# Attention steps of a fused attention and mixture kernel: weighted sums and output transposes ahead of the query transposes, which get two PSUM banks of their own

## The chip, the core and the metric

The kernel runs on one core of one Trainium2 chip. The metric is device time in microseconds; three runs of the kernel before took 1943.64 to 1944.79 us, with a median of 1944.15 us. A profile records one further execution. Engines are called TensorE (PE in the rows; PEld are its weight loads), VectorE (DVE), ScalarE (ACT), GpSimd (POOL) and SyncE (SP, which here issues loads and stores).

## What is computed

Three layers follow each other: linear attention with an exponential feature map, then a mixture of experts with soft weights, then one in which each token goes to one expert. The change touches the first alone:

```python
def _attn_ref(q, k, v, w_phi):
    def phi(x):
        proj = np.einsum('bhsd,df->bhsf', x, w_phi)
        proj = proj - np.max(np.abs(proj), axis=-1, keepdims=True)
        return np.concatenate([np.exp(proj), np.exp(-proj)], axis=-1)
    q_p, k_p = (phi(q), phi(k))
    kv = np.einsum('bhsf,bhsd->bhfd', k_p, v)
    z = np.sum(k_p, axis=2)
    num = np.einsum('bhsf,bhfd->bhsd', q_p, kv)
    den = np.einsum('bhsf,bhf->bhs', q_p, z)[..., None] + 1e-06
    return num / den
```

with 4 batches, 8 heads, 576 positions, 64 values per head and 128 features, all in float32.

## The kernel before

Attention's work is cut into 8 units (two batches and two heads each) of 3 groups; a group is 3 chunks of 128 positions for both heads. The order is written out by hand: the loop from line 651 calls `step` once per group (step i takes group i as keys), and each engine executes its instructions in the order of these calls. Each group passes through a pipeline:

- `proj` (L138) multiplies a group of keys (step i) or queries (two steps later) by the feature matrix on TensorE (L144, row tiles of 64), and VectorE takes the largest magnitude (L149) and subtracts it (L150; `mk`, `prk` for keys, `mq`, `prq` for queries). For keys ScalarE takes both exponentials at once (`ek`, L154).
- `kvm` (L159), one step later, sums the products of key features and values in two banks, psC and psB (L170, column tiles of 64). It issues 24 matmuls, or 32 in the middle group of a unit, where a chunk spans two batches (steps 5, 8, 11, ..., 23). Each float32 matmul stands in the profile as two weight loads and two matmuls, except transposes: 48 or 64 records. After the last group of a unit `kvcopy` copies the sums out (ScalarE).
- `qtr` (L178), one step after a query's projection, transposes it (6 transposes, L184), and ScalarE takes the exponentials (`eq`, L187).
- `num` (L190), one step after that, makes the weighted sums and their denominators (L198, 48 records, column tiles of 64). VectorE divides: an addition, a reciprocal and a multiply (L201 to L203; the multiply writes `xn`). This document calls these three the division.
- `xtr` (L206), again one step later, transposes the quotient (3 transposes, L211), ScalarE copies it out (`xo`, L213) and SyncE stores it.

PSUM has 8 banks. Tiles psR (two banks each, two buffers) serve the key projection, the query projection and the query transposes in turn; psD (one bank, two buffers) serves weighted sums and output transposes; psC and psB hold the key-value sums. Steps from i = 25 on, the tail, run in a new pool, whose first tiles psC and psB lie on the old pool's first two banks and where each user has tiles of its own; there the first matmuls of the next layer (`more`) are put between the parts. Small VectorE work (`misc_comp`) is called ahead of steps 6 and later, four transposes of the expert embedding (`misc_trans`, L296) after step 11, and background work (`bg`: weight and input splits on ScalarE and GpSimd) after the steps from 12 on.

Of the kernel before, what the change touches and what calls it, by code (L numbers as in the profile page):

```python
# [11 lines left out]
F32 = mybir.dt.float32  # L12
# [9 lines left out]
B, H, S, D = 4, 8, 576, 64  # L22
NT = B * S
DM = H * D
E, FF = 8, 1024
P = 128
NTL = NT // P
KD = DM // P
# [16 lines left out]
def build(tc, a, out):  # L45
# [5 lines left out]
    live = {}  # L51
# [9 lines left out]

    n_ps = [0]

    def psum(tag, shape):
        n_ps[0] += 1
        bufs = {"A": 4, "B": 1, "C": 1, "D": 2}[tag]
        return live["pp"].tile(shape, F32, tag="ps" + tag, bufs=bufs, name=f"ps{tag}{n_ps[0]}")
# [31 lines left out]
    NG, NC = len(CH), len(CH[0])  # L99
    GW = NC * P  # L100
    S2 = 2 * S
    W = D + 1
# [13 lines left out]

    def heads2(tags):
        if not live.get("tail"):
            n_ps[0] += 1
            t = live["pp"].tile([P, 2, 512], F32, tag="psR", bufs=2, name=f"psR{n_ps[0]}")[:, :, 0:GW]  # L120
            return [t[:, 0], t[:, 1]], [(slice(0, 2), t)]
        ts = [psum(t_, [P, 1, GW]) for t_ in tags]
        return [t[:, 0] for t in ts], [(slice(h_, h_ + 1), t) for h_, t in enumerate(ts)]

    def warm(n):
        ps = psum("D", [P, P])
        for _ in range(n):
            T.matmul(ps, ident, ident, start=True, stop=True)

# [4 lines left out]
    load_in(0, "k", 1)  # L134
    load_v(0)
    warm(10)

    def proj(u, which, g):  # L138
        r = live.pop(("r" + which, u, g))
        hs, parts = heads2("CB")  # L140
        for c in range(NC):
            for h_ in range(2):
                rs = slice(h_ * D, h_ * D + D)
                T.matmul(hs[h_][:, c * P:(c + 1) * P], r[rs, c * P:(c + 1) * P], wphi[rs, :], start=True, stop=True)  # L144
        m = ap_.tile([P, 2, NC], F32, tag="m", bufs=4, name=f"m{which}{u}{g}")
        pr = ap_.tile([P, 2, NC, P], F32, tag="pr" + which, name=f"pr{which}{u}{g}")
        for h_, ps in parts:
            ps = ps.rearrange("p h (c f) -> p h c f", f=P)
            V.tensor_reduce(out=m[:, h_], in_=ps, axis=AX.X, op=ALU.max, apply_absolute_value=True)  # L149
            V.tensor_tensor(out=pr[:, h_], in0=ps, in1=m[:, h_].unsqueeze(3).to_broadcast([P, h_.stop - h_.start, NC, P]), op=ALU.subtract)  # L150
        if which == "k":
            ek = ap_.tile([P, 2, 2, NC, P], F32, tag="ek", name=f"ek{u}{g}")
            for sg in range(2):
                A.activation(out=ek[:, sg], in_=pr, func=AF.Exp, scale=1.0 - 2.0 * sg)  # L154
            live["ek", u, g] = ek
        else:
            live["pr", u, g] = pr

    def kvm(u, g):  # L159
        v, ek = live["v", u], live.pop(("ek", u, g))  # L160
        if g == 0:
            live["kv", u] = [psum(t, [P, 2, 2 * W]) for t in "CB"]
        for ci, c in enumerate(CH[g]):
            for sg in range(2):
                for h_ in range(2):
                    ps = live["kv", u][h_]
                    for s0 in (c,) if c < 4 else (4, 5) if c == 4 else (c + 1,):
                        o = W * (s0 > 4)
                        for cs in HALVES:
                            T.matmul(ps[cs, sg, o:o + W], ek[:, sg, h_, ci, cs], v[:, h_, s0 * W:s0 * W + W], start=(c == 0 and sg == 0), stop=(c == 8 and sg == 1))  # L170

    def kvcopy(u):
        kvz = ap_.tile([P, 2, 2, 2 * W], F32, tag="kvz", name=f"kvz{u}")
        for h_, ps in enumerate(live.pop(("kv", u))):
            A.copy(kvz[:, h_], ps)
        live["kvz", u] = kvz

    def qtr(u, g):  # L178
        pr = live.pop(("pr", u, g))
        eq = ap_.tile([P, 2, 2, GW], F32, tag="eq", name=f"eq{u}{g}")  # L180
        hs, parts = heads2("DD")
        for h_ in range(2):
            for c in range(NC):
                T.transpose(hs[h_][:, c * P:(c + 1) * P], pr[:, h_, c, :], ident)  # L184
        for sg in range(2):
            for h_, ps in parts:
                A.activation(out=eq[:, sg, h_], in_=ps, func=AF.Exp, scale=1.0 - 2.0 * sg)  # L187
        live["eq", u, g] = eq

    def num(u, g):  # L190
        eq, kvz = live.pop(("eq", u, g)), live["kvz", u]
        ps = psum("C" if live.get("tail") else "D", [P, 2 * NC, W])
        for ci, c in enumerate(CH[g]):
            for h_ in range(2):
                for sg in range(2):
                    for i, cs in enumerate(HALVES):
                        o = W * (2 * c + i > 8)
                        T.matmul(ps[cs, 2 * ci + h_, :], eq[:, sg, h_, ci * P + cs.start:ci * P + cs.stop], kvz[:, h_, sg, o:o + W], start=(sg == 0), stop=(sg == 1))  # L198
        d = ap_.tile([P, 2 * NC], F32, tag="d", name=f"d{u}{g}")
        xn = ap_.tile([P, 2 * NC, D], F32, tag="xn", name=f"xn{u}{g}")  # L200
        V.tensor_scalar_add(d, ps[:, :, D], 1e-6)  # L201
        V.reciprocal(d, d)
        V.tensor_tensor(out=xn, in0=ps[:, :, 0:D], in1=d.unsqueeze(2).to_broadcast([P, 2 * NC, D]), op=ALU.mult)  # L203
        live["xn", u, g] = xn

    def xtr(u, g):  # L206
        bp, h_ = units[u]
        xn = live.pop(("xn", u, g))
        ps = psum("B" if live.get("tail") else "D", [P, GW])
        for c in range(NC):  # L210
            T.transpose(ps[:, c * P:(c + 1) * P], xn[:, 2 * c:2 * c + 2, :].rearrange("p h e -> p (h e)"), ident)  # L211
        xo = ap_.tile([P, GW], F32, tag="xo", name=f"xo{u}{g}")
        A.copy(xo, ps)  # L213
        o = bp * S2 + g * GW
        SP.dma_start(out=xd[:, h_, o:o + GW], in_=xo)
# [75 lines left out]
        V.tensor_scalar_mul(emb, emb, es)  # L291

    def misc_trans():
        ps = psum("D", [P, KD, E])
        for k in range(KD):
            T.transpose(ps[:, k, :], emb[:, k * P:(k + 1) * P], ident[0:E, 0:E])  # L296
        V.tensor_copy(enT, ps)
# [313 lines left out]
    def step(k, q, fill=None):  # L611
        def more(n=1):
            for _ in range(n if fill else 0):
                filled[0] += 1
                next(fill)

        ko, qo, no, xo_ = (pipe[c] for c in "kqnx")
        pipe.update(k=k, q=q, n=qo, x=no)
        if k:
            proj(k[0], "k", k[1])  # L620
        if q:
            proj(q[0], "q", q[1])
        more()
        if ko:
            kvm(*ko)
        if qo:
            qtr(*qo)
        if ko and ko[1] == NG - 1:
            kvcopy(ko[0])
        more()  # L630
        if xo_:
            xtr(*xo_)
        if no:
            num(*no)
        more()

    misc = misc_comp()
# [13 lines left out]
    while i < NU * NG + LAG or any(pipe.values()):  # L651
        p, g = divmod(i, NG)
# [24 lines left out]
        if i == NU * NG + 1:  # L677
# [4 lines left out]
            o2 = wops(2, 0, {"A21": "S3"})  # L682
            bg.extend(o2[nm] for nm in ("A11", "A12", "A21", "A22"))
        step(at_(i), at_(i - LAG), first if i > NU * NG else None)
        if i == 11:
            misc_trans()
# [326 lines left out]
    def route_steps(t0, ta, tl, **rest):  # L1013
        fns = dict(p=route_p, b=route_b, o=route_o, c=route_c, s=route_s, d=route_d, w=route_w)
        ev = [(k, partial(route_l, t0, i)) for i, k in enumerate(tl)] + [(k, partial(route_a, t0, i, "D" if k % 40 < 13 else "B")) for i, k in enumerate(ta)]
        ev += [(k, partial(fns[nm], t0)) for nm, k in rest.items() if nm != "i"]
        return ev + [(k, partial(route_i, t0, i)) for i, k in enumerate(rest["i"])]
# [248 lines left out]
    tail = route_steps(0, (1, 2, 4, 6, 8, 10), (1, 2, 3, 4, 5, 6), b=8, o=9, p=11, c=12, s=13, d=14, w=15, i=(16, 16, 18, 19, 20, 21))  # L1266
# [152 lines left out]
    more = nc.values_load(total, min_val=0, max_val=NBLK)  # L1419
# [83 lines left out]
```

## Time and profile before

| what | value |
|---|---|
| three runs, median | 1944.15 us (1943.64 to 1944.79) |
| the profiled execution | 1945.93 us, of which its span is 1944.1 us |
| TensorE busy | 1896.0 us, 98% of the span |
| VectorE busy | 1269.1 us, 65% |
| ScalarE busy | 850.6 us, 44% |
| GpSimd busy | 935.0 us, 48% |
| attention with its tail | the first 180 us of the span, about |

Busy times are sums over records; matmuls overlap each other in the engine, so TensorE's figure says that it was rarely empty, not that it ran at its peak. A row of the timeline gives the start in us, the time from the start of its first to the end of its last instruction, the engine, the line, the operation, the tiles it writes and reads, the shape, the number of instructions, and in brackets the idle time of its engine before it and what ended that.

### The profile page before, as it was taken

The numbers are of one execution on the slowest core, as the hardware profiler recorded it, in microseconds if no ns is written. First come the engines' busy times: TensorE is split into PE (matmuls) and PEld (weight loads), VectorE is DVE, ScalarE is ACT, GpSimd is POOL, SyncE is SP. The second block draws the span as 40 slices with busy tenths as digits, with TensorE's granted clock in tenths as the row PEclk, the third lists the DMA queues.
The fourth block names the chain that finished last, engine by engine and source line by source line (L and its number), as shares of the span: only waits on it lengthen the run. The fifth ranks groups of instructions, "written<-read, shape, count | busy, mean of one in ns | idle before, by whom it ended". The sixth has DMA issues, their size and how long they took to land.

```text
span 1944.1 us, 33725 instructions
## 1 busy us (share of the span) xinstructions
PE 1896.0 (98%) x13210; PEld 1809.0 (93%) x13210; DVE 1269.1 (65%) x1671; ACT 850.6 (44%) x1255; POOL 935.0 (48%) x667
## 2 busy tenths in 40 slices
PE   8999999999999999999999999999999997899998
PEld 7898999999999999999999999999999986688886
DVE  6775564657657556567566566566566446799995
ACT  4574431323333333424333333334233234688885
POOL 0241034847466564747475665748474434442221
PEclk9999999999999999999999999999999999899999
DMA  4474634345362726354353727264453354153851
GB/s 150 149 262 171 240 142 164 138 149 174 122 215 105 251 81 235 111 184 168 128 190 107 243 91 251 91 209 132 164 173 122 131 187 109 50 192 112 324 208 40
DMA packets 121445, 314.23 MB, mean 162 GB/s; under 512 B 20136, under 2 KB 68408, under 8 KB 121282
## 3 DMA queue, kind: packets, MB, share of 16 engines
q1 hardware_dynamic: 117186, 301.51, 45.7%
q0 software_dynamic: 4096, 10.51, 1.8%
q8 instruction: 107, 1.75, 0.4%
q14 instruction: 56, 0.46, 0.1%
HBM read 335.27 MB, written 32.28 MB: 189 GB/s over the span
## 4 chain that ended last, share of the span: by engine, by line
PE 73%; POOL 11%; issue 7%; DVE 5%; DMA 2%; ACT 2%; SPq 1%; POOLq 0%; DVEq 0%; ACTq 0%
PE Q L407 14%; PE Q L408 14%; PE Q L406 14%; POOL w1S L326 2%; POOL hB L454 2%; PE psD L406 2%; PE psD L407 2%; PE psD L408 2%; PE psA L406 2%; POOL hT L454 2%; PE psA L408 2%; PE psA L407 2%; PE psA L1105 2%; PE psA L1106 2%; PE psA L1104 2%
## 5 line engine op out<-in xcount | busy, mean ns | idle before, releaser
L470 DVE TENSOR_TENSOR acca<-acca,Q 128x768 f32<-128x768 f32 x182 | 168.5, 949 | 133.1 <-PE Q L408 133.1
L406 PE MATMUL Q<-hT,w2S 128*128 128x384 f32 x468 | 157.4, 336 | 4.1 <-DVE rd L466 4.1
L454 POOL TENSOR_TENSOR hB<-rb,hB 128x768 fp32r<-128x768 f32 x39 | 72.1, 1848 | 180.7 <-ACT hB L451 180.7
L406 PE MATMUL Q<-xT,w1S 128*128 128x384 f32 x468 | 156.5, 334 | 0.9 <-ACT ra L475 0.9
L407 PE MATMUL Q<-hT,w2S 128*128 128x384 f32 x468 | 156.4, 334 | 0.0
L408 PE MATMUL Q<-hT,w2S 128*128 128x384 f32 x468 | 156.4, 334 | 0.0
L407 PE MATMUL Q<-xT,w1S 128*128 128x384 f32 x468 | 156.3, 334 | 0.0
L408 PE MATMUL Q<-xT,w1S 128*128 128x384 f32 x468 | 156.3, 334 | 0.0
L326 POOL TENSOR_TENSOR w1A<-raw,w1A 128x512 fp32r<-128x512 f32 x48 | 62.0, 1292 | 180.8 <-ACT w1A L325 106.9
L470 DVE TENSOR_TENSOR accb<-accb,Q 128x768 f32<-128x768 f32 x91 | 84.2, 949 | 68.1 <-PE Q L408 68.1
L466 DVE TENSOR_TENSOR Q<-Q,ra 128x768 f32<-128x768 f32 x39 | 37.7, 966 | 123.9 <-PE Q L408 123.9
L1078 DVE TENSOR_TENSOR s1l<-rw,s1h 128x1024 fp32r<-128x1024 f32 x88 | 104.7, 1243 | 10.5 <-ACT s1h L1077 9.4
L475 ACT COPY ra<-Q 128x768 f32<-128x768 f32 x39 | 31.2, 800 | 175.1 <-PE Q L408 155.4
L408 PE MATMUL Q<-hB,w2A 128*128 128x384 f32 x312 | 104.3, 334 | 0.0
L406 PE MATMUL Q<-xB,w1A 128*128 128x384 f32 x312 | 104.2, 334 | 0.0
L407 PE MATMUL Q<-hB,w2A 128*128 128x384 f32 x312 | 104.2, 334 | 0.0
L407 PE MATMUL Q<-xB,w1A 128*128 128x384 f32 x312 | 104.2, 334 | 0.0
L408 PE MATMUL Q<-xB,w1A 128*128 128x384 f32 x312 | 104.2, 334 | 0.0
L406 PE MATMUL Q<-hB,w2A 128*128 128x384 f32 x312 | 104.2, 334 | 0.0
L454 POOL TENSOR_TENSOR hT<-ra,hT 128x768 fp32r<-128x768 f32 x39 | 71.8, 1842 | 64.3 <-ACT hT L451 64.3
L1145 POOL DMA_INDIRECT out<-y,idt x22 | 25.0, 1137 | 161.0 <-ACT y L1144 150.7
L454 POOL TENSOR_TENSOR hT<-rd,hT 128x768 fp32r<-128x768 f32 x39 | 72.3, 1854 | 57.2 <-ACT hT L451 57.2
(421 smaller groups left out, 6280.2 us busy)
## 6 DMA issues: line engine op xcount, KB each, us to landing
xT<-xpd SPq DMA_DIRECT2D x120, 768.0 KB
rw<-in_moe_w SPq DMA_DIRECT2D x176, 512.0 KB
xB<-xpd SPq DMA_DIRECT2D x90, 768.0 KB
raw<-in_moe_w SPq DMA_DIRECT2D x34, 512.0 KB
gate<-gd SPq DMA_DIRECT2D x45, 384.0 KB
rx<-in_moe_w SPq DMA_DIRECT2D x30, 512.0 KB
xpd<-xT SPq DMA_DIRECT2D x12, 768.0 KB
xpd<-xB SPq DMA_DIRECT2D x9, 768.0 KB
```

The lines of the kernel that those rows point to most:

```text
L326: eng.tensor_tensor(out=t[:, 1], in0=r(nm), in1=f32(t[:, 0]), op=ALU.subtract)
L406: T.matmul(bank, w[:, 0, j, k, :], x[:, 0, k, :], start=start and k == 0, stop=False, skip_group_check=True)
L407: T.matmul(bank, w[:, 0, j, k, :], x[:, 1, k, :], start=False, stop=False, skip_group_check=True)
L408: T.matmul(bank, w[:, 1, j, k, :], x[:, 0, k, :], start=False, stop=stop and k == 1, skip_group_check=True)
L454: eng.tensor_tensor(out=hb[nm][:, 1], in0=src, in1=f32(hb[nm][:, 0]), op=ALU.subtract)
L466: V.tensor_tensor(out=out, in0=x, in1=y, op=op)
L470: V.tensor_tensor(out=z, in0=z, in1=ps, op=op)
L475: A.copy(m1c, b0)
L1078: eng.tensor_tensor(out=lo, in0=r, in1=f32(hi), op=ALU.subtract)
L1104: T.matmul(ps[hf], th[:, k, :], wh[:, cs], start=(k == 0), stop=False)
L1105: T.matmul(ps[hf], tl[:, k, :], wh[:, cs], start=False, stop=False)
L1106: T.matmul(ps[hf], th[:, k, :], wl[:, cs], start=False, stop=(k == KD - 1))
```

## The change

In a step, `kvm` and `kvcopy` are now followed by `num`, then `xtr`, then `qtr` (before: `qtr`, `kvcopy`, `xtr`, `num`). The query transposes write a tile psQ of two banks with one buffer. The weighted sums take bank 0 of a psR tile, and the output transposes bank 1 of the same tile. The warm-up matmuls and the embedding transposes, which used psD, use psQ. The tail keeps its tiles, but has the new order too.

```diff
+    def two_banks(tag, bufs):
+        n_ps[0] += 1
+        return live["pp"].tile([P, 2, 512], F32, tag="ps" + tag, bufs=bufs, name=f"ps{tag}{n_ps[0]}")
+
...
     def heads2(tags):
         if not live.get("tail"):
-            n_ps[0] += 1
-            t = live["pp"].tile([P, 2, 512], F32, tag="psR", bufs=2, name=f"psR{n_ps[0]}")[:, :, 0:GW]
+            t = (two_banks("Q", 1) if tags == "DD" else two_banks("R", 2))[:, :, 0:GW]
             return [t[:, 0], t[:, 1]], [(slice(0, 2), t)]
...
     def warm(n):
-        ps = psum("D", [P, P])
+        ps = two_banks("Q", 1)[:, 0, 0:P]
...
     def num(u, g):
         eq, kvz = live.pop(("eq", u, g)), live["kvz", u]
-        ps = psum("C" if live.get("tail") else "D", [P, 2 * NC, W])
+        if live.get("tail"):
+            ps = psum("C", [P, 2 * NC, W])
+        else:
+            live["nx"] = two_banks("R", 2)
+            ps = live["nx"][:, 0, 0:2 * NC * W].rearrange("p (c w) -> p c w", w=W)
...
-    def xtr(u, g):
+    def xtr(u, g, no):
         bp, h_ = units[u]
         xn = live.pop(("xn", u, g))
-        ps = psum("B" if live.get("tail") else "D", [P, GW])
+        ps = psum("B", [P, GW]) if live.get("tail") else (live.get("nx") if no else None) or two_banks("R", 2)
+        ps = ps if live.get("tail") else ps[:, 1, 0:GW]
...
     def misc_trans():
-        ps = psum("D", [P, KD, E])
+        ps = two_banks("Q", 1)[:, 0, 0:KD * E].rearrange("p (k e) -> p k e", e=E)
...
         if ko:
             kvm(*ko)
+        if ko and ko[1] == NG - 1:
+            kvcopy(ko[0])
+        if no:
+            num(*no)
+        more()
+        if xo_:
+            xtr(*xo_, no)
         if qo:
             qtr(*qo)
-        if ko and ko[1] == NG - 1:
-            kvcopy(ko[0])
-        more()
-        if xo_:
-            xtr(*xo_)
-        if no:
-            num(*no)
         more()
```

TensorE before, from the last key-value sums of step 17 to the projections of step 18; names in brackets are the semaphores that an instruction waits for (DVE, PE, Activation and DMAHW stand for VectorE, TensorE, ScalarE and a load):

```order
L170 MATMUL psB_1678<-v_1320,ek_1663 64x65 x2
L184 MATMUL psR_1818<-ident,prq_1674 128x128 [waits DVE_49,PE_49]
L184 MATMUL psR_1818<-ident,prq_1674 128x128 x5
L211 MATMUL psD_1827<-ident,xn_1746 128x128 [waits Activation_49]
L211 MATMUL psD_1827<-ident,xn_1746 128x128 x2
L198 MATMUL psD_1834<-kvz_1602,eq_1703 64x65 x24
L144 MATMUL psR_1881<-wphi,rk_1646 128x128 [waits DMAHW6_49,DVE_49,PE_49]
L144 MATMUL psR_1895<-wphi,rq_1648 128x128 [waits DMAHW7_49,PE_49,Activation_49]
```

Of VectorE the query transposes wait here for the subtraction of this step's key projection, which used their buffer.

TensorE with the change, the same place (lines are those of the changed kernel: 205 weighted sums, 219 output transposes, 187 query transposes, 147 projections):

```order
L173 MATMUL psB_1667<-v_1312,ek_1652 64x65 x2
L205 MATMUL psR_1805<-kvz_1582,eq_1728 64x65 [waits DVE_49,PE_49,Activation_49]
L205 MATMUL psR_1805<-kvz_1582,eq_1728 64x65 [waits Activation_49]
L205 MATMUL psR_1805<-kvz_1582,eq_1728 64x65 x21
L219 MATMUL psR_1805<-ident,xn_1718 128x128 [waits DVE_49]
L219 MATMUL psR_1805<-ident,xn_1718 128x128 x2
L187 MATMUL psQ_1842<-ident,prq_1663 128x128 x6
L147 MATMUL psR_1868<-wphi,rk_1635 128x128 [waits DMAHW6_49,PE_49]
L147 MATMUL psR_1882<-wphi,rq_1637 128x128 [waits DMAHW7_49,Activation_49]
```

The weighted sums, moved ahead of both transposes, carry the wait for the key projection's subtraction. The output transposes have a wait on VectorE that they did not have; the count that it names is the one that the multiply of this step's division reaches (it reads psR_1805, bank 0, and writes the next `xn`), not the multiply that wrote xn_1718. The same holds in each of the 20 steps, 5 to 24, that transpose outputs ahead of the tail. ScalarE's order in a step changes from `eq`, `kvcopy`, `xo` to `kvcopy`, `xo`, `eq`; the orders on VectorE, GpSimd and SyncE stay as they were.

TensorE with the change, from the last query transposes ahead of the tail to the tail's first projection:

```order
L187 MATMUL psQ_2587<-ident,prq_2428 128x128 [waits PE_49]
L187 MATMUL psQ_2587<-ident,prq_2428 128x128 x5
L147 MATMUL psC_2600<-wphi,rq_2404 128x128 [waits DMAHW1_49,PE_49,Activation_49]
```

and before, from the last weighted sums ahead of the tail:

```order
L198 MATMUL psD_2586<-kvz_2270,eq_2481 64x65 x23
L144 MATMUL psC_2620<-wphi,rq_2422 128x128 [waits DMAHW1_49,DVE_49,PE_49]
L144 MATMUL psB_2621<-wphi,rq_2422 128x128 [waits Activation_49]
```

The tail's psC and psB lie where the old pool's first two banks were: psD before (last read by the division and the output copy), psQ now, last read by the exponentials of step 24.

## Rows read from the trace of the kernel before

**Rows 1.** Busy time by stretch: start:end, length, busy and (records) by engine, granted clock, DMA share.
```profile
20.00:152.00 132.00, 127.03 (x2864) 116.85 (x2860) 99.38 (x167) 84.25 (x136) 34.29 (x23) 1.00 0.56 189
8.00:11.00 3.00, 0.73 (x14) 0.40 (x10) 2.93 (x4) 1.38 (x2) 0.00 (x0) 0.99 0.79 240
11.00:14.00 3.00, 2.75 (x44) 2.63 (x46) 0.44 (x1) 1.77 (x3) 0.00 (x0) 0.50 0.53 128
1635.00:1640.00 5.00, 3.29 (x33) 2.78 (x32) 2.44 (x4) 4.59 (x9) 0.18 (x1) 1.00 0.27 68
```

**Rows 2.** What TensorE waited for from 20 to 152 us: total, times, longest.
```profile
PE psR L184 <- DVE prk L150: 2.2, 4, 0.8
PE psR L144 <- DMA rk<-in_kT: 0.8, 1, 0.8
```

**Rows 3.** Timeline of TensorE's weight loads: step 17's key-value sums, then all of step 19.
```profile
104.99 0.20 PEld L170 LDWEIGHTS psC<-v,ek 128*64 128x64 f32 x4
...
107.01 0.64 PEld L184 LDWEIGHTS psR<-ident,prq 128*128 128x128 f32 x6
...
113.97 1.48 PEld L198 LDWEIGHTS psD<-kvz,eq 128*64 128x64 f32 x48 [0.17 <-issue]
115.51 0.75 PEld L144 LDWEIGHTS psR<-wphi,rk 64*128 64x128 f32 x12
116.18 0.75 PEld L144 LDWEIGHTS psR<-wphi,rq 64*128 64x128 f32 x12
117.05 0.20 PEld L170 LDWEIGHTS psC<-v,ek 128*64 128x64 f32 x4
...
118.33 0.20 PEld L170 LDWEIGHTS psB<-v,ek 128*64 128x64 f32 x4
118.66 0.64 PEld L184 LDWEIGHTS psR<-ident,prq 128*128 128x128 f32 x6
119.26 0.36 PEld L211 LDWEIGHTS psD<-ident,xn 128*128 128x128 f32 x3
119.79 1.48 PEld L198 LDWEIGHTS psD<-kvz,eq 128*64 128x64 f32 x48 [0.17 <-issue]
121.34 0.19 PEld L144 LDWEIGHTS psR<-wphi,rk 64*128 64x128 f32 x2
```

**Rows 4.** Timeline of VectorE in step 19.
```profile
115.63 0.17 DVE L201 TENSOR_SCALAR d<-psD 128x6 f32<-128x6 f32 x1 [1.06 <-PE psD L198]
...
116.06 0.56 DVE L203 TENSOR_TENSOR xn<-psD,d 128x384 f32<-128x384 f32 x1
116.53 0.95 DVE L149 TENSOR_REDUCE mk<-psR 128x6 f32<-128x768 f32 x1
117.58 0.96 DVE L150 TENSOR_TENSOR prk<-psR,mk 128x768 f32<-128x768 f32 x1
...
119.44 0.96 DVE L150 TENSOR_TENSOR prq<-psR,mq 128x768 f32<-128x768 f32 x1
```

**Rows 5.** Timeline around the first query transposes, step 3.
```profile
21.33 0.64 PEld L184 LDWEIGHTS psR<-ident,prq 128*128 128x128 f32 x6
...
21.63 0.96 DVE L150 TENSOR_TENSOR prq<-psR,mq 128x768 f32<-128x768 f32 x1
22.31 1.49 ACT L187 ACTIVATE eq<-psR 128x768 f32<-128x768 f32 x2
```

**Rows 6.** Timeline around the embedding transposes, after step 11.
```profile
73.60 0.32 PEld L296 LDWEIGHTS psD<-ident,embt 8*128 8x128 f32 x4 [0.67 <-ACT xo L213]
...
73.94 0.75 PEld L144 LDWEIGHTS psR<-wphi,rk 64*128 64x128 f32 x12
...
74.93 0.96 DVE L149 TENSOR_REDUCE mk<-psR 128x6 f32<-128x768 f32 x1 [0.69 <-PE psR L144]
```

**Rows 7.** Timeline of step 24 and the tail's first projection.
```profile
146.44 0.75 PEld L144 LDWEIGHTS psR<-wphi,rq 64*128 64x128 f32 x12
...
152.71 0.18 PEld L144 LDWEIGHTS psC<-wphi,rq 64*128 64x128 f32 x1 [1.24 <-issue]
```

## The prediction

> **What bounds the kernel now.** I read the busy times by stretch first, then TensorE's waits, then one step of the attention stage record by record. In the stretch from 20 to 152 us, nearly all of attention, TensorE is busy for 127.03 of 132 us at a granted clock of 1.00 (2.4 GHz), VectorE for 99.38 and ScalarE for 84.25 [rows 1]. What TensorE waited for there is little: 2.2 us for the subtraction of a key projection, 0.8 us for one load of keys [rows 2]. So the stage is bound by TensorE's own stream, and the question is what each step of that stream costs. The reader is to see in one step (step 19) that its weight loads follow one another almost without a hole: key projection at 115.51, query projection at 116.18, key-value sums at 117.05, query transposes at 118.66, output transposes at 119.26, weighted sums at 119.79, next key projection at 121.34: a step of 5.83 us [rows 3]. And that VectorE runs close beside it: the division that follows the weighted sums (lines 201 to 203) runs from 115.63 to 116.62, the key reduction and subtraction from 116.53 to 118.54, the query's to 120.40 [rows 4]. Before, this division had a whole step to be ready: the output transposes that read its result come one step later and write another tile.
>
> **The change, part by part.** The instructions and their sizes are the same, DMAs too; their order on TensorE and ScalarE, their PSUM tiles and their waits are new. Times below count from a step's first key-projection load.
>
> *Fewer switches of shape.* Key-value sums and weighted sums, both with 64-column weights, now follow each other. Forty-four loads of the former take 1.28 us (117.05 to 118.33), so 48 take 1.40 and 64 take 1.86 [rows 3]. The gap at a switch is what is left over: 1.55 - 1.40 = 0.15 us from weighted sums to projection; 1.13 for nine transposes of 0.10 us each, so 0.23, from output transposes to weighted sums; 0.87 - 0.67 = 0.20 from projection to key-value sums [rows 3]. Four switches a step become three. The new one, from query transposes to key projection, is in no row; I take 0.23, the switch that also leaves transposes, with 0.15 as the other end. The Trainium skill states the reason on its page "TensorEngine Tiling (Array Packing)", section "Key Properties": a change of tiling mode drains the engine. By that rule alone the change saves one switch a step, 3 to 4 us in all; the holes in the trace agree that switches cost time, but the next two points are larger.
>
> *The weighted sums wait where the query transposes waited.* Tiles psR rotate over two buffers and three users a step, so the third user takes the key projection's buffer and waits for its subtraction. With VectorE free, the key reduction starts 0.99 us after the first load (73.94 to 74.93) [rows 6]; from its start to the end of the subtraction are 2.01 us, and TensorE's next load comes 0.12 us after that end (118.54 to 118.66) [rows 3, 4]. That makes 3.12, against 1.54 + 1.40 = 2.94 without a wait. With 64 key-value loads it is 1.54 + 1.86 = 3.40 and nothing is waited for.
>
> *The output transposes now wait for the division of their own step.* This is the term that decides. They write bank 1 of the tile whose bank 0 holds this step's weighted sums. The built program puts a wait on VectorE before the first of them (the order in the section on the change), for the count that this step's multiply reaches, although they read the multiply of the step before. From the first load of the weighted sums to the start of the division are 1.66 us (113.97 to 115.63), from there to its end 0.99 [rows 3, 4]. So the division starts at 3.12 + 1.66 = 4.78; VectorE is free by then, since the query's subtraction ends 3.87 us after the key reduction's start, at 4.86, and a record starts some 0.09 us before the end of the one ahead of it (116.53 against 116.62) [rows 4]. It ends at 5.77, the transposes start at 5.89, and behind them in TensorE's queue stand the query transposes and both projections of the next step. Nine transposes and a switch take 1.13 us: the next step starts at 7.02 instead of 5.83. With 64 key-value loads the same sum is 3.40 + 1.66 + 0.99 + 0.12 + 1.13 = 7.30.
>
> *The query transposes in their own tile psQ.* At the start this helps: the query projection no longer waits for ScalarE to empty a shared tile. In step 3 the transposes load at 21.33; step 4 can start at 21.33 + 0.60 + 0.23 = 22.16, its query projection at 22.83 (the subtraction it needs ends at 22.59), its weighted sums at 22.16 + 3.12 = 25.28 with no output transposes yet, so step 5 starts at 25.28 + 1.55 + 0.83 = 27.66, about 1 us earlier [rows 3, 5]. At two places it costs. The embedding transposes after step 11 share psQ: they need the exponentials of that step, which start 0.98 us after the transposes' first load and take 1.49 [rows 5]; with 0.12 for the handover and 0.34 for themselves (73.60 to 73.94) [rows 6] the next step starts 2.93 us after that load instead of 0.83, so 2.1 more. And the first projection of the tail waits for the exponentials of step 24 (its wait on ScalarE stands in the order). Step 24 has no key projection: weighted sums at 0.87 + 1.40 = 2.27, division from 3.93 to 4.92, output transposes at 5.04, query transposes at 5.34, exponentials done at 5.34 + 0.98 + 1.49 = 7.81, tail at 7.93; before it was 152.71 - 146.44 = 6.27 [rows 7].
>
> *ScalarE and the loads* I cost at nothing. ScalarE now does the output copy before the query exponentials; these end 0.12 + 0.30 + 0.98 + 1.49 us after the division, 1.6 us into the next step, and are wanted at 3.12. If that cover were gone, the weighted sums would be late by the difference. The queue of loads keeps its order and gets more time per step. The small VectorE work of steps 6 to 11 falls into the 1.25 us between the division's end and the next step's start.
>
> *Sum.* Steps 5 to 23 are 12 of the short and 7 of the long kind: 12 x 7.02 + 7 x 7.30 = 135.3. With 27.66 at the start, 2.1 after step 11 and 7.93 for step 24 the tail starts at 173.0 instead of 152.7 [rows 7], which is **20.3 us later**. In the tail every user has a tile of its own as before; I cost it at nothing (0 to 0.6). What follows is released by attention's end and moves with it. The profiled execution took 1945.93 us and would take 1966.2; it stands 1.78 us above the median of the runs, 1944.15, so the runs would have 1964.5 (1964.45). Bounds: the new switch at 0.15 takes off 1.6; another 0.1 us of wait per step would add 2.
>
> **The rivals.**
> *No wait for the own step's division.* If the transposes waited only for the older multiply, a short step would be 3.12 + 1.55 + 1.13 = 5.80, a long one 6.08, step 24 by the same sums 6.7, and the tail would start at 148.6, 4.1 earlier, if no load were late. But one load of keys was already 0.8 late [rows 2] and would be so again, and by some 0.3 more (an estimate: what the five steps ahead of it gain), so 1944.15 - 4.1 + 1.1 = 1941.2: not slower. It decides as soon as that wait is met before 4.67, the end of the weighted sums. For it speaks that the two banks share no data; against it, that the wait stands in the program on all 20 steps that transpose outputs ahead of the tail. The Trainium skill's page "PSUM — Partial Sum Buffer", section "🎯 Summary: rules for kernel authors", asks only for a different bank when PSUM is read while matmuls run; by that rule the chip would need no such wait, and the result would be this rival's time. The wait is the program's, so I give it little.
> *The clock falls.* TensorE now stands idle for about 1.2 us in each step. From 11 to 14 us the granted clock was 0.50 (1.2 GHz), after 3 us in which TensorE was busy for 0.73 [rows 1]. If it fell in each of the 19 steps for as long, 3 us at half the rate would cost 1.5 us a step: 1964.5 + 28 = 1993. Against it: from 1635 to 1640 us TensorE was busy for only 3.29 of 5 us, and the clock stayed at 1.00 [rows 1]; the new step keeps it busy for 5.8 of 7.02.
>
> **How the numbers follow.** Forecast 0.87, its own range 1962 to 1968; no wait 0.05; clock 0.05; other 0.03. A difference below 0.2%, 3.9 us, counts as none. I widen the range to 1958 to 1971 for terms that repeat 19 times and are known to 0.1 us; it leaves out both rivals. Slower by over 0.2%: 0.94. Within it: 0.04, most of the first rival. Faster: 0.02.
>
> **What would show it.** Right: at the head of TensorE's waits stand the output transposes behind this step's multiply on VectorE, 20 times, about 1.2 us each; key projections follow at 7.0 and 7.3 us; the embedding transposes wait some 2 us for ScalarE; the tail starts near 173 us; the clock stays at 2.4 GHz and everything after attention keeps its length. Wrong: steps of 5.8 us without that wait, a granted clock below 1.00 between 20 and 170 us, or a difference that arises after attention.

## The result, and the profile after

Five runs of the changed kernel have a median of **1966.72 us** (1964.04 to 1970.49), against 1944.15 before: 1.0122 of before, 95% interval [1.0108, 1.0136], 22.6 us slower. The forecast was 1964.5 with a range of 1958 to 1971. A second comparison gave 1965.65 against 1946.29, ratio 1.0098 [1.0081, 1.0114]. The profiled execution took 1970.49 us, the slowest of the five, with a span of 1968.7.

The views of after, in the order of the rows of before. Busy time by stretch: length, busy time and (records) of TensorE, its weight loads, VectorE, ScalarE, GpSimd, then granted clock, DMA share and GB/s.

```profile
20.00:152.00 132.00, 111.99 (x2445) 102.78 (x2441) 88.02 (x148) 74.70 (x116) 25.30 (x18) 0.97 0.45 149
```

TensorE was busy for 127.03 us of that stretch before [rows 1] and is busy for 111.99 now: it does less in the same time, because it waits and, as shown below, because its clock falls for a while. What it waits for from 20 to 175 us (total, times, longest):

```profile
PE psR L219 <- DVE xn L210: 20.5, 19, 1.1
PE psQ L304 <- ACT eq L190: 1.7, 1, 1.7
PE psC L147 <- ACT eq L190: 1.7, 1, 1.7
PE psR L219 <- DVE wgt L296: 1.1, 1, 1.1
```

None of these stands in [rows 2]; the waits that stood there are gone. Line 219 is the output transposes, line 210 the multiply that ends the division: 20 waits together (in the last row another small VectorE instruction is named, the place is the same), 21.6 us. Step 19 by its weight loads, to be read beside [rows 3]:

```profile
130.61 0.75 PEld L147 LDWEIGHTS psR<-wphi,rk 64*128 64x128 f32 x12 [0.17 <-issue]
131.28 0.75 PEld L147 LDWEIGHTS psR<-wphi,rq 64*128 64x128 f32 x12
...
133.74 1.51 PEld L205 LDWEIGHTS psR<-kvz,eq 128*64 128x64 f32 x48
136.46 0.31 PEld L219 LDWEIGHTS psR<-ident,xn 128*128 128x128 f32 x3 [1.21 <-DVE xn L210]
136.73 0.69 PEld L187 LDWEIGHTS psQ<-ident,prq 128*128 128x128 f32 x6
137.59 0.52 PEld L147 LDWEIGHTS psR<-wphi,rk 64*128 64x128 f32 x8 [0.17 <-issue]
```

And on VectorE, beside [rows 4]:

```profile
131.60 0.96 DVE L152 TENSOR_REDUCE mk<-psR 128x6 f32<-128x768 f32 x1 [2.17 <-PE psR L147]
...
134.52 0.96 DVE L153 TENSOR_TENSOR prq<-psR,mq 128x768 f32<-128x768 f32 x1
135.42 0.16 DVE L208 TENSOR_SCALAR d<-psR 128x6 f32<-128x6 f32 x1
...
135.85 0.56 DVE L210 TENSOR_TENSOR xn<-psR,d 128x384 f32<-128x384 f32 x1
```

The weighted sums load at 3.13 us into the step, the division starts at 4.81 and ends at 5.80, the transposes load at 5.85, the next step starts at 6.98. VectorE, which ran close beside TensorE before, now stands idle for 2.17 us ahead of each key reduction of a short step, because the key projection that it waits for stands in TensorE's queue behind the transposes that wait for VectorE's own division.

At the start, beside [rows 5], psQ helps: step 4 begins 0.80 us after the query transposes' first load, where it was 1.33 (21.33 to 22.66).

```profile
16.57 0.75 PEld L147 LDWEIGHTS psR<-wphi,rk 64*128 64x128 f32 x12
...
20.41 0.64 PEld L187 LDWEIGHTS psQ<-ident,prq 128*128 128x128 f32 x6
21.21 0.75 PEld L147 LDWEIGHTS psR<-wphi,rk 64*128 64x128 f32 x12 [0.17 <-issue]
...
26.72 0.75 PEld L147 LDWEIGHTS psR<-wphi,rk 64*128 64x128 f32 x12 [0.16 <-issue]
```

The other two waits are those of psQ, at the embedding transposes after step 11 (where [rows 6] showed 0.67) and at the tail's first projection [rows 7]. They are followed by a fall of the granted clock to half, which the trace of before shows in attention only from about 11 to 14 us [rows 1] and nowhere from 20 to 190 us. First the loads around the two places, then the stretches ahead of and behind them:

```profile
75.51 0.69 PEld L187 LDWEIGHTS psQ<-ident,prq 128*128 128x128 f32 x6
...
78.10 0.50 PEld L304 LDWEIGHTS psQ<-ident,embt 8*128 8x128 f32 x4 [1.90 <-ACT eq L190]
...
166.12 0.75 PEld L147 LDWEIGHTS psR<-wphi,rq 64*128 64x128 f32 x12 [0.17 <-issue]
...
171.37 0.69 PEld L187 LDWEIGHTS psQ<-ident,prq 128*128 128x128 f32 x6
173.96 0.28 PEld L147 LDWEIGHTS psC<-wphi,rq 64*128 64x128 f32 x1 [1.90 <-ACT eq L190]
```

```profile
75.00:78.00 3.00, 1.20 (x9) 0.97 (x9) 0.18 (x1) 1.95 (x3) 0.00 (x0) 0.99 0.21 72
78.00:84.00 6.00, 5.90 (x74) 5.65 (x76) 3.73 (x5) 1.62 (x3) 0.00 (x0) 0.50 0.20 65
...
173.00:174.00 1.00, 0.04 (x2) 0.04 (x2) 0.00 (x0) 0.91 (x2) 0.00 (x0) 0.74 0.67 252
174.00:180.00 6.00, 6.00 (x60) 5.34 (x62) 2.14 (x4) 0.48 (x1) 0.00 (x0) 0.50 0.01 3
```

From 75 to 78 us TensorE worked for 1.20 of 3 us; the next 6 us stand at 0.50 (1.2 GHz). The same happens at 174. The tail starts at 173.96 instead of 152.71, 21.3 us later. Matched instruction by instruction, the two traces are 24.1 us apart at 184 us. At the first matmuls of the next layer some of this is given back, since the kernel before waited there for ScalarE longer than the changed one does (first row before, second after):

```profile
PE psD L406 <- ACT accb L816: 1.2, 1, 1.2
PE psD L414 <- ACT accb L824: 0.2, 1, 0.2
```

From 305 to 1500 us the distance is 22.8 us, which is what the medians differ by. At the change from the second layer to the third it grows to the 24.6 by which the spans differ at the end; the experiments show that this place varies by itself.

### The profile page after: what moved, and what is told of

It reads as the page before. It is cut to its first block, busy times and chain, and to the rows that moved or that the text cites. A ratio compares the mean times of both kernels' runs of the same rounds, so it can differ in the third digit from the quotient of the medians.

```text
span 1968.7 us, 33736 instructions
## 1 busy us (share of the span) xinstructions
PE 1903.2 (97%) x13210; PEld 1814.6 (92%) x13210; DVE 1270.0 (65%) x1671; ACT 855.1 (43%) x1255; POOL 935.0 (47%) x667
## 4 chain that ended last, share of the span: by engine, by line
PE 72%; POOL 9%; DVE 7%; issue 6%; DMA 3%; ACT 2%; SPq 1%; POOLq 0%; DVEq 0%; ACTq 0%
PE Q L415 15%; PE Q L416 15%; PE Q L414 15%; PE psD L414 2%; PE psD L415 2%; PE psD L416 2%; PE psA L414 2%; PE psA L416 2%; PE psA L415 2%; POOL w1S L334 2%; POOL hB L462 2%; PE psD L1147 1%; PE psD L1146 1%; PE psD L1145 1%; PE psA L1113 1%
```

## The experiments

The theory: the tile that the weighted sums and the output transposes share makes the transposes wait for the division, and psQ makes two other users wait for exponentials. The rival for the first: the new order itself costs the time. Step lengths below are distances between the first loads of successive key projections; "short" steps have 48 loads of key-value sums, "long" ones 64.

**The output transposes in a tile of their own.**

```diff
     def xtr(u, g, no):
-        ps = psum("B", [P, GW]) if live.get("tail") else (live.get("nx") if no else None) or two_banks("R", 2)
+        ps = psum("B", [P, GW]) if live.get("tail") else two_banks("R", 2)
```

> The changed kernel, but the output transposes take a psR tile of their own instead of bank 1 of the weighted sums' tile; order unchanged. Theory (the 1.2 us per step are the wait for the own step's division, and that wait comes from the shared tile): the transposes wait only for the query subtraction, some 4.98 us into the step, and the next key projection for the output copy (transposes + 1.11 + 0.12), so a short step takes 6.2 us instead of 6.98, a long one 6.2 instead of 7.24, and step 24 about 1.1 less: 12 x 0.77 + 7 x 1.04 + 1.1 = 17.6 us less than the changed kernel's 1966.7, 1949.1. Rival (the new order or the query transposes' tile costs it, by shape switches or by what stands behind them): steps stay within 0.2 us of 6.98 and the time at 1963 to 1967.

Measured: 1948.01 us (1945.09 to 1949.18), 1.0004 of the kernel before [0.9994, 1.0014]. Steps of 6.14 us, short and long alike. The waits of the same stretch:

```profile
PE psR L219 <- DVE d L208: 2.8, 12, 0.2
PE psQ L304 <- ACT eq L190: 1.7, 1, 1.7
PE psC L147 <- ACT eq L190: 1.7, 1, 1.7
```

The 20 long waits have become 12 of 0.2 us, with the order untouched. The shared tile is shown to be the cause, and the order by itself is not: one line brings the kernel from 1.0122 of before to 1.0004. What the new tile waits for instead is seen in one step, which starts at 109.21:

```profile
113.12 0.96 DVE L153 TENSOR_TENSOR prq<-psR,mq 128x768 f32<-128x768 f32 x1
114.02 0.17 DVE L208 TENSOR_SCALAR d<-psR 128x6 f32<-128x6 f32 x1
```

```profile
112.33 1.51 PEld L205 LDWEIGHTS psR<-kvz,eq 128*64 128x64 f32 x48
114.19 0.31 PEld L219 LDWEIGHTS psR<-ident,xn 128*128 128x128 f32 x3 [0.35 <-PE psR L205]
114.47 0.69 PEld L187 LDWEIGHTS psQ<-ident,prq 128*128 128x128 f32 x6
115.35 0.30 PEld L147 LDWEIGHTS psR<-wphi,rk 64*128 64x128 f32 x4 [0.20 <-ACT xo L221]
```

The query subtraction ends at 114.08 and the transposes load 0.11 later, 4.98 us into the step, as expected. The views put this wait down to other instructions (a later VectorE record, or TensorE itself); the two times tell what it was.

**The query transposes ahead of the output transposes.**

```diff
+        early = not live.get("tail")
+        exps = qtr(*qo) if qo and early else None
         if xo_:
             xtr(*xo_, no)
-        if qo:
-            qtr(*qo)
+        if qo and not early:
+            exps = qtr(*qo)
+        if exps:
+            exps()
```

Here `qtr` returns its two exponentials as a function (that part of the edit is left out above), which is called last, so that ScalarE's order stays; in the tail TensorE's order is that of the changed kernel.

> The changed kernel, but on TensorE the query transposes stand ahead of the output transposes (ScalarE's order is kept: output copy, then exponentials); tiles unchanged. Theory (the wait ends at a fixed point, the end of the division 5.85 us into the step, whatever stands in front): the six query transposes fill 0.6 us of the wait, so steps of 6.38 and 6.64 us, 18 of them 0.6 shorter, 10.8 us less: 1955.9. Embedding transposes and tail still wait for exponentials and gain 0.1 each. Rival (the cost is a drain or switch around the output transposes, not a wait for VectorE): step lengths unchanged, 1966.7.

Measured: 1954.91 us (1949.31 to 1957.88), 1.0043 [1.0032, 1.0054]. Steps of 6.33 and 6.60. What TensorE waits for:

```profile
PE psR L222 <- DVE xn L213: 5.2, 19, 0.3
PE psQ L307 <- ACT eq L192: 2.0, 1, 2.0
PE psC L147 <- ACT eq L192: 2.0, 1, 2.0
PE psR L222 <- DVE wgt L299: 0.3, 1, 0.3
```

The same wait, 0.3 instead of 1.1 us: it ends at a fixed point, and work put in front of it is free. The two waits for exponentials grew from 1.7 to 2.0 us. Step 12 took 7.67 us where the changed kernel had 9.59, which was not expected: the fall of the clock behind the embedding transposes was shorter.

**The order alone.** The kernel before, with the `step` of the changed one; psD and psR as before.

> The kernel before with the new order alone: weighted sums and output transposes in psD tiles of one bank each, query transposes in psR. Theory: no wait for the own step's division, but the query projection of the next step takes the buffer of the query transposes and waits for their exponentials (transposes at 4.79, exponentials 5.77 to 7.26, projection at 7.38 instead of 6.29): steps of 6.7 us, 7.2 with 64 key-value loads, embedding transposes without a wait, no fall of the clock there: about 1958, 14 slower than before. Rival (the order by itself saves a switch per step and nothing waits): steps of 5.6 us and 1940.

Measured: 1956.34 us (1955.90 to 1961.69), 1.0056 [1.0034, 1.0078]. Steps of 6.68 and 7.15.

```profile
PE psR L144 <- ACT eq L187: 15.7, 20, 1.1
PE psA L406 <- ACT eq L187: 0.7, 1, 0.7
```

With the old tiles the new order waits too, 20 times, but for ScalarE: the query projection takes the buffer that the query transposes have just filled. So the tile psQ was a real remedy for a real wait of the new order; what cost the time was where the weighted sums and the output transposes went.

**The embedding transposes in psR.** Twice, in two comparisons.

```diff
     def misc_trans():
-        ps = two_banks("Q", 1)[:, 0, 0:KD * E].rearrange("p (k e) -> p k e", e=E)
+        ps = two_banks("R", 2)[:, 0, 0:KD * E].rearrange("p (k e) -> p k e", e=E)
```

> The changed kernel, but the embedding transposes after step 11 take a psR tile instead of psQ. Theory (the extra 2.3 us of step 11 are their wait for the exponentials, and the 6.3 us at half clock that follow in step 12 come from that longest idle time): step 11 takes 7.24 + 0.5 = 7.8 instead of 9.50, step 12 6.98 instead of 9.59, the granted clock stays at 1.00 from 20 to 165 us: 4.3 us less, 1962.4. Rival (the clock falls from idle time summed over the steps): the fall comes in another step, and only 1.7 us are saved, 1965.0.

Measured: 1962.26 us (1961.25 to 1963.51), 1.0080 [1.0062, 1.0097]. Step 11 takes 7.58 us instead of 9.50, step 12 6.99 instead of 9.59, and the other steps from the fifth on are unchanged. Of the 4.5 us, 1.9 were the wait and 2.6 the half clock behind it. The 2.6 is the most that was seen: in the other four profiles with this wait step 12 is 1.0 to 1.4 us above a short step of the same kernel. Its stretch from 75 to 90 us stands at full clock, where the changed kernel had 6 us at 0.50:

```profile
75.00:90.00 15.00, 12.85 (x274) 11.63 (x274) 9.39 (x15) 8.69 (x15) 3.78 (x3) 1.00 0.40 125
```

**And the warm-up in psR.** This shifts psR to the first four banks, so that the tail's first tile no longer lies on psQ.

```diff
     def warm(n):
-        ps = two_banks("Q", 1)[:, 0, 0:P]
+        ps = two_banks("R", 2)[:, 0, 0:P]
```

> The changed kernel with the embedding transposes in psR and the warm-up in psR alone; order and the shared tile of weighted sums and output transposes stay. Theory: against the run with the embedding transposes moved (1962.3) the tail's first projection no longer waits 1.7 us for exponentials, and the half clock behind it (174 to 180 us, worth 2.8 in the tail) goes: 1957.8, with all 19 steps unchanged at 6.98 and 7.24. Rival (that fall of the clock does not come from this wait): 1960.6.

Measured: 1962.60 us (1961.69 to 1963.11), 1.0082 [1.0066, 1.0097]. A miss. In attention the theory held: the tail starts at 166.29 instead of 168.20, and the clock behind it stays up (from 165 to 190 us 1.00, against 0.93 with the embedding transposes alone moved). But the expected 4.5 us did not arrive at the end. Set side by side instruction by instruction, the trace with both edits is 3.3 us ahead at 185 us: 0.2 of that stood there before the tail, 1.7 are the wait and 1.4 the clock, which the expectation had at 2.8. It is 3.6 us ahead at 1600 us, level at about 1653 and 1.9 us behind at the end: the gain was lost where the first of the two expert layers ends and the second begins.

```profile
1640.00:1690.00 50.00, 39.99 (x273) 33.20 (x272) 27.80 (x49) 27.11 (x43) 14.33 (x12) 0.90 0.43 132
```

```profile
1640.00:1690.00 50.00, 39.79 (x252) 32.67 (x251) 26.91 (x46) 27.06 (x43) 13.46 (x11) 0.80 0.42 111
```

The first row is the embedding transposes alone, the second both edits: a granted clock of 0.90 against 0.80. To tell whether the earlier start brings this about or chance does, three kernels were profiled again, and the first of the two once more after that.

> The changed kernel once more, in the same comparison as the two others, for a second profile. If the two falls of the clock in attention (78 to 84.3 us, and 174 to 180 us) come from the waits for exponentials ahead of them, both are there again at the same places, step 12 takes 9.6 us again and the tail starts at 174.0; if they come by chance, at least one is gone. The stretches at half clock from 1640 to 1730 us may stand elsewhere. Time 1967, 21 to 22 above the kernel before.

> The kernel with the embedding transposes and the warm-up in psR once more. The first time its tail began 1.9 us earlier than with the embedding transposes alone moved, at full clock, and its time was the same; 20.5 us at half clock stood between 1635 and 1690 us, against 13.6. If that number varies from execution to execution, it will differ here and the time with it, 1959 to 1963; if the earlier start brings it about, it is 20.5 again and the time 1962.5.

> The kernel before, unchanged, for a second profile. Steps of 5.83 and 6.24 us and a tail from 152.7 us again, within 0.3. If the time at half clock near the change of layer varies by itself, it is not 10.2 us from 1590 to 1680 us as it was, and the span moves by half the difference.

> The kernel with the embedding transposes alone in psR once more, for a second profile against the two of the kernel with the warm-up in psR as well (20.5 us at half clock between 1640 and 1690 us in both, 1962.6 and 1962.2). If the change of layer differs from execution to execution whatever the tail's start, this profile may show 17 to 20 us at half clock there too and a span 2 to 4 us longer than the first's 1959.4, and the tail starts at 168.2 again with a fall of the clock behind it. If the tail's later start is what keeps that stretch short, it is 13.6 again.

Measured: the changed kernel 1965.65 us; step 11 9.48, step 12 8.13, the tail at 173.12, both falls of the clock at the same places, each about half as long as the first time. Both edits 1962.18 us (1959.33 to 1962.93), clock 0.80 again in that stretch. The kernel before 1946.44, 1.0002 [0.9992, 1.0012], steps as before, with a span of 1940.1 instead of 1944.1: 2.3 us of that stand there before step 3, which began at 15.20 instead of 17.49, with no fall of the clock in the first 20 us. The embedding transposes alone 1963.87 us (1963.19 to 1964.51), 1.0091 [1.0076, 1.0105], and its row of that stretch is no longer the one above:

```profile
1640.00:1690.00 50.00, 38.05 (x253) 32.00 (x252) 25.63 (x39) 25.96 (x42) 13.48 (x11) 0.83 0.48 127
```

The two profiles of this kernel stand some 0.1 us apart from 1000 to 1626 us and 2.7 apart at the end. So that stretch, where TensorE is busy for 38 to 40 of 50 us, comes out differently from one execution to the next, by as much as the tail's wait costs. In this second profile there was also no fall of the clock at the tail, though the wait of 1.7 us stood there. Against its two times (1962.26, 1963.87) the earlier tail (1962.60, 1962.18) is worth about 0.7 us, which these runs can hardly tell from nothing. In the second pair of profiles the one with both edits is 0.9 us ahead at the end, 0.8 of which it had before the tail. Whether the earlier tail itself brings on part of the loss stays open.

**Own tile and query transposes first, together.**

> Both edits at once: output transposes in a psR tile of their own, and the query transposes ahead of them on TensorE. Theory: nothing on TensorE waits long for the own step's division any more; the next key projection takes the weighted sums' buffer and waits for the multiply, which ends about when TensorE comes there (5.85 us into the step). Steps of 5.87 and 6.13 us, 1.1 less than the changed kernel's in 19 steps (21 us) and 0.7 each less at step 11 and step 24: 1944.4, level with the kernel before; the waits of the embedding transposes and of the tail's first projection for exponentials stay. Rival (new order has a cost of its own beyond these waits): 1948 or more, as with the own tile alone.

Measured: 1948.38 us (1945.11 to 1952.57), 1.0011 [1.0002, 1.0020]; in that comparison the kernel before stood at 1946.38. Short and long steps of 5.88 and 6.16, as expected. The time is not: 2 us above before, and 4 above the forecast. The tail begins at 152.36, which looks like 0.35 us ahead of before, but step 3 began at 15.63 where it began at 17.49 in the first profile of before and at 15.20 in the second. From step 3 to the tail it is 136.73 us, against 135.22 and 135.05, and set beside the second profile of before the trace is 2.2 to 2.5 us behind from 171 to 1500 us, about what the medians differ by. So the loss arises in attention. Step 12 with its wait and its fall of the clock (7.24 us) was part of what stayed; steps 19, 20 and 22 took 6.37, 7.10 and 6.95 us, 2.5 us over. In step 22 a load of queries came 1.0 us late:

```profile
PE psR L147 <- DMA rq<-in_qT: 1.0, 1, 1.0
```

This is the kind of loss that the first rival of the prediction had for keys. In steps 19 and 20 TensorE stood idle at the weighted sums (0.39 and 0.84 us by the weight loads); the views do not settle what held them.

**All these waits off.** The two edits just named, the embedding transposes in psR and the warm-up in psR.

> The same, and also: the embedding transposes take a psR tile, and the warm-up matmuls take psR instead of psQ, so that psR lies on the first four banks and the tail's first two tiles lie where the output transposes were and not on psQ. Theory: the waits for exponentials after step 11 (1.7) and at the tail (1.5) go, and with them what the clock took behind them (1 to 2.6 each): 6 to 8 us less than with both edits alone, 1936 to 1938, which is below the kernel before. Rival (the clock falls elsewhere, or a load of keys comes late): 1941.

Measured: 1942.73 us (1941.23 to 1945.04), 0.9984 of before [0.9975, 0.9993], 3.65 us faster. What TensorE still waits for from 20 to 175 us:

```profile
PE psC L147 <- ACT xo L224: 0.6, 1, 0.6
PE psR L147 <- ACT eq L192: 0.5, 1, 0.5
PE psR L147 <- DVE enT L308: 0.3, 1, 0.3
PE psB L173 <- issue: 0.2, 1, 0.2
```

The clock is 1.00 from 20 to 190 us and the tail starts at 146.88, 5.8 us ahead of the first profile of before. But 2.2 of that stood there at step 3 (15.30 against 17.49), ahead of the first query transposes, where both kernels do the same work. From step 3 to the tail it takes 131.58 us, against 135.22 and 135.05: 3.5 to 3.6 less, which is the whole 3.65 of the medians. The expectation was 6 to 8 us less than with the two edits alone, and it was 5.65 less than their 1948.38; the forecast of 1936 to 1938 was missed because that run stood 4 above its own. It is the only version here that beats the kernel before, and by less than the 0.2% that counted as a difference.

## Why the prediction was right

It was right in sign, in the mechanism that decides and, partly by luck, so nearly in size: a cost that it left out was made up in part by an earlier start. By its own steps:

*The wait for the own step's division.* Right to 0.06 us: short steps of 6.98 (forecast 7.02), long ones 7.24 (7.30), 20 waits. The rival without that wait fell with the waits in the trace of after, and the run that took the tile away and kept the order shows that the tile is what brings the wait. The Trainium skill's page "PSUM — Partial Sum Buffer", section "🎯 Summary: rules for kernel authors", asks for a different bank while PSUM is read. Here another bank was given and the transposes still waited 1.1 us in each of 20 steps, and with another tile they did not. That is a wait of the built program, which follows tiles; whether the chip would have allowed both banks at once, no run here shows.

*The weighted sums* start 3.13 us into a short step (forecast 3.12). *Fewer switches:* from the query transposes' first load to the next key projection it is 0.86 us (136.73 to 137.59), and the forecast's 0.60 + 0.23 was 0.83. The Trainium skill's page "TensorEngine Tiling (Array Packing)", section "Key Properties", says that a change of tiling mode drains the engine; the hole of 0.26 us that is left beside the 0.60 of the transposes is in keeping with that. No run singles out what the saved switch is worth; against switches of 0.15 to 0.26 us the wait of 1.1 us is four times as much or more.

*The start.* Step 5 begins 10.15 us after step 3 (16.57 to 26.72), where 10.17 was forecast. That it begins at 26.72 and not at 27.66 comes from ahead of step 3, which began at 16.57 instead of 17.49; in the second profile of the kernel before it began at 15.20. So the beginning of an execution varies by 2 us by itself, and these 0.92 us are chance.

*The embedding transposes:* 2.26 us (9.50 - 7.24) for 2.1. *Step 24:* 7.84 for 7.93. The tail at 173.96 for 173.0.

**What failed** is a term that was left at nothing: the clock behind the two long waits. The rival had priced a fall of the clock in each of 19 steps; none came there. It came after the two waits for exponentials, which the forecast had named and priced without it: 2.6 us in step 12, and some 2.7 us in the tail, where the delay grows from 21.3 us at its start to 24.1 at 184 us (it grew by 0.2 there in the run that had neither the wait nor the fall). A granted clock below 1.00 between 20 and 170 us was one of the prediction's own signs of being wrong; it came at 78 us, for a reason that the prediction did not have, while the wait that it rested on was there as forecast. The terms that came out short (0.94 at the start, 12 x 0.04 and 7 x 0.06 in the steps, 1.8 together) hid a third of it. That what follows moves with attention's end was right to about 1 us: of the 24.1 us 1.3 were given back by 305 us, and 1.8 came on at the change of layer. So the profiled execution took 1970.49, where the sum made against it had 1966.2. In the second profile the falls were half as long, and there the tail began at 173.12 and the execution took 1965.89.

*ScalarE and the loads at nothing* held: no load was late, no wait of the weighted sums for exponentials shows.

## What to carry to other kernels

Two users in two banks of one tile are one user to the program's waits: before moving operations into a shared allocation, list for each half which engine's last reader the next writer will be made to wait for, and how far away that reader is in the new order. A wait that ends at a fixed point costs only the part of it that no independent work fills: putting the query transposes ahead of it gave back 0.6 us a step. And when a bound engine is made to wait, price the clock behind the longest wait too, not only the wait. Last, before reading a gain off two profiles, subtract what they differ by ahead of the change: here the start alone moved by up to 2.3 us.

## What the runs showed of the hardware

In the steps of the changed kernel TensorE was busy for 27.69 of 32 us, a wait of 1.1 us in every step included, and kept a granted clock of 1.00; a single longer wait that left it at 1.20 of 3 busy us was followed by 6 us at 0.50.

```profile
88.00:120.00 32.00, 27.69 (x629) 25.37 (x629) 20.97 (x31) 20.65 (x33) 12.69 (x11) 1.00 0.43 136
```

The embedding transposes' wait (1.7 to 2.0 us) was followed by such a fall in all five profiles that had it, and with these transposes in another tile the fall at that place was gone in all five profiles of such kernels. The tail's wait of the same length was followed by one in five of seven. Of the six profiles without either wait (the kernel before twice, the order alone, the one with all waits off and the two with the warm-up moved) none shows a fall between 20 and 190 us. Why the tail's wait was not followed by one in the two others stays open. From 1640 to 1690 us, near the change of layer, the same kernel's clock stood at 0.90 in one profile and at 0.83 in the next, and its span differed by 2.7 us, which arose there: one profile is not enough to judge an edit worth 2 us there.
